# Probabilities of the second batch transposed by TensorE instead of VectorE, in an attention and two-MoE kernel

## The chip, the core and the metric

The kernel runs on one core of one Trainium2 chip. The metric is the device time of one execution in microseconds (us), as the median of several runs; smaller is better. All engines of the core (TensorE or PE, its weight loads PEld, VectorE or DVE, ScalarE or ACT, GpSimd or POOL, and SyncE or SP, which issues the transfers) run their own instruction streams in order and meet through semaphores.

## What is computed

Three stages follow each other. The pooled attention has 8 batches, 8 heads, 576 tokens and a head dimension of 64, and its keys and values are means of 8 neighbouring tokens, so each token attends to 72 positions. Then come two feed-forward stages over 4608 tokens of width 512. All of it is in float32; the weights of the stages arrive as float64.

```python
k_p = k.reshape(B, H, Sp, 8, D).mean(axis=3)
v_p = v.reshape(B, H, Sp, 8, D).mean(axis=3)
scores = (1 / sqrt(D)) * q @ k_p.T
attn = exp(scores - max(scores)); attn = attn / (sum(attn) + 1e-9)
x = (attn @ v_p) -> (4608, 512)
x2 = ((x @ w1) * (x @ w2)) @ w3 @ w_out
h = x2 @ w_in2;  out = (h * sigmoid(1.702 * h)) @ w_out2
```

## The kernel before

The heads are worked on in pairs: a group is one batch and two heads, so there are 32 groups, four to a batch, numbered n = 0 to 31. A group goes through small functions, each given out at one tick of a counter, four ticks to a group:

- `g0` (line 251) transposes keys and queries by DVE blocks and pools the keys.
- `g1` (line 263) makes the scores: five pairs of matmuls on line 271 into the two PSUM banks `wk[2]` and `wk[3]`, a maximum by DVE (line 276) and a subtraction (line 278) into `s_t`, a tile of 128 tokens by 5 token tiles by 160 columns, of which 144 hold the 2 x 72 scores.
- `g2` (line 285) is the exponential on ACT.
- `g3` (line 288) sums and normalizes the probabilities on DVE (lines 292 to 295). Then the matmul that follows needs them with the 144 positions on partitions. For a group n that is not below `NPE`, `g3` does this itself by 20 DVE instructions (line 306), each turning blocks of 32 x 32, from `s_t` to `p0` (the first 128 positions) and `p1` (the last 16, padded to 32). For n below `NPE` it returns on line 301.
- `g4` (line 337) does the same for n below `NPE` by ten PE transposes against an identity (lines 343, 346, 348, 352 and 353) into `wk[2]` and `wk[3]`, with four ACT copies (lines 344, 350, 351 and 354) from there to `p0` and `p1`. For every group it then splits `p0` and `p1` into a high and a low part in the reduced format that PE takes (lines 360 to 364, ACT and POOL).
- `g6` (line 366) multiplies by the pooled values, two halves of 288 tokens, into `wk[2]` and `wk[3]`, and writes the high part (ACT, line 382) and the low part (DVE, line 383) of the result to the slots of `x`.

The ticks have this order: tick 4n gives `g4(n-1)`, tick 4n+1 `g1(n)`, tick 4n+2 `g6(n-1)`, `g2(n)`, `g_va(n)` and `g0(n+1)`, tick 4n+3 `g3(n)` and `g_vb(n)`. A setup phase converts the float64 weights (lines 166 to 174) and multiplies `w3` by `w_out` (one matmul for all tokens instead of two); it gives out ticks 0 to 19, which carry groups 0 to 3 to their end and group 4 through `g3`. Then nine blocks of 512 tokens follow. A block has eight steps f; each step is 24 matmuls of 512 columns into `wk[0]` and `wk[1]` (lines 113 to 115, called from line 585), a copy of `wk[0]` by ACT (line 599), the product by DVE (line 602), the split of it, and 12 matmuls into `acc` for an earlier step (line 550), with two ticks in between. So block 0 carries groups 4 to 7, which are batch 1, from `g4(4)` to `g6(7)`; block 1 needs them. Block 0 itself needs groups 0 to 3. Matmuls on lines 113 to 115 are triples of high and low parts: high by high, high by low, low by high. The `w_in2` and `w_out2` stage comes after the nine blocks.

A framework sets the semaphores, and orders the instructions of each engine ahead of time by the priority of the program's order and by its own simulated times; the order on the chip is then fixed. Tiles of one PSUM bank are handed from one user to the next in program order, so `g1(n+1)` takes `wk[2]` and `wk[3]` after the last reader of `g4(n)`, where that used them.

Of the kernel before, what the change touches and what calls it, by code (L numbers as in the profile page):

```python
# [22 lines left out]
def pooled_attention_moe_moe2(  # L23
# [26 lines left out]
    HP = H // 2  # L50
# [2 lines left out]
    NF2 = DF2 // P  # L53
    NB = NT // T
    NG = B * HP
    NPE = HP
    SB = S // 32
    TT = (S + P - 1) // P
    KW = 2 * SK
# [133 lines left out]
    with pa_ctx:  # L193
# [94 lines left out]
        def g3(n):  # L288
# [10 lines left out]
            g_s[n] = (p0, p1)  # L299
            if n < NPE:  # L300
                return
# [35 lines left out]
        def g4(n):  # L337
            p0, p1 = g_s.pop(n)
            if n < NPE:
                ps = wk[2:]  # L340
# [573 lines left out]
```

## Time and profile before

| what | us |
|---|---|
| median of 3 runs | 1552.37 (1552.19 to 1552.53) |
| the profiled execution | 1552.57 |
| its span, first to last instruction | 1550.9 |
| PE busy | 1491.6 |
| DVE busy | 983.4 |
| ACT busy | 618.6 |
| POOL busy | 590.1 |

The profile gives each engine's busy time, a table of stretches with each engine's busy time and PE's granted clock (1.00 is 2.4 GHz, 0.50 is 1.2 GHz), a timeline of instructions, and for each idle time of an engine what ended it. Matmuls are pipelined: the duration of one is longer than the distance from its start to the next one's, so PE's cost is read from starts.

### The profile page before, as it was taken

How to read it: one execution, taken by the hardware profiler on the slowest of the kernel's cores; microseconds unless marked ns; L12 is line 12 of the kernel's file. 1: busy time of each engine (PE TensorE's matmuls, PEld its weight loads, DVE VectorE, ACT ScalarE, POOL GpSimd, SP SyncE). 2: the span in 40 equal slices, each digit the busy share in tenths (PEclk: the TensorE clock that was granted, in tenths of full speed). 3: DMA queues.
4: the chain of work that ended last, by engine and by line, in shares of the span. 5: the costliest groups of instructions: out<-in, count | busy, mean ns of one | idle time of the engine just before them, and what ended most of it. 6: DMA issues, size and time to landing. Idle time of an engine off the chain costs nothing.

```text
span 1550.9 us, 19562 instructions
## 1 busy us (share of the span) xinstructions
PE 1491.6 (96%) x6728; PEld 1230.2 (79%) x6728; DVE 983.4 (63%) x1810; ACT 618.6 (40%) x1202; POOL 590.1 (38%) x660
## 2 busy tenths in 40 slices
PE   5975999999999999999999999999999999999998
PEld 4653888888888888887878888888888888888887
DVE  8999988787877877669554244463447253734441
ACT  6774444334344333366553222342225222522231
POOL 7788755555555555359472211101110011101110
PEclk9876999999999999999999999999999999999999
DMA  9971233223232320089879243323343233423310
GB/s 273 248 174 37 57 60 74 54 67 68 59 67 53 74 47 36 27 277 368 347 255 380 89 150 129 128 84 134 111 136 109 102 124 115 150 74 123 129 48 28
DMA packets 225444, 196.33 MB, mean 127 GB/s; under 512 B 158784, under 2 KB 175168, under 8 KB 225344
## 3 DMA queue, kind: packets, MB, share of 16 engines
q1 hardware_dynamic: 224768, 194.03, 40.7%
q8 instruction: 53, 0.87, 0.2%
q10 hardware_dynamic: 576, 1.05, 0.2%
q14 instruction: 47, 0.39, 0.1%
HBM read 150.99 MB, written 44.04 MB: 126 GB/s over the span
## 4 chain that ended last, share of the span: by engine, by line
PE 85%; DVE 8%; DMA 2%; issue 2%; SPq 1%; POOL 1%; ACT 1%; DVEq 0%; POOLq 0%
PE bk L682 22%; PE bk L114 8%; PE bk L115 8%; PE bk L113 8%; PE wk L113 7%; PE wk L115 7%; PE wk L114 7%; PE acc L113 4%; PE acc L115 4%; PE acc L114 4%; PE wk L271 2%; DVE cv L171 1%; DVE s L104 1%; DVE cv L168 1%; DMA s<-in_moe_w_dram 1%
## 5 line engine op out<-in xcount | busy, mean ns | idle before, releaser
L682 PE MATMUL bk<-xM,st 128*128 128x512 f32 x1080 | 261.3, 389 | 0.0
L682 PEld LDWEIGHTS bk<-xM,st 128*128 128x128 f32 x1080 | 202.6, 188 | 42.5 <-ACT o L699 0.4
L113 PE MATMUL wk<-s,s 128*128 128x512 f32 x576 | 228.1, 398 | 6.1 <-ACT s L382 3.7
L114 PE MATMUL wk<-s,s 128*128 128x512 f32 x576 | 226.4, 394 | 4.1 <-DVE s L383 4.1
L115 PE MATMUL wk<-s,s 128*128 128x512 f32 x576 | 225.8, 393 | 1.4 <-DVE s L104 1.4
L114 PE MATMUL bk<-wo,mv 128*128 128x512 f32 x576 | 224.1, 389 | 0.0
L113 PE MATMUL bk<-wo,mv 128*128 128x512 f32 x576 | 223.9, 389 | 0.0
L115 PE MATMUL bk<-wo,mv 128*128 128x512 f32 x576 | 209.9, 389 | 0.0
L306 DVE STREAM_TRANSPOSE p<-s_t 32x160 f32<-32x160 f32 (+1 forms) x560 | 178.6, 319 | 11.0
L818 POOL TENSOR_TENSOR s<-s,sg 128x512 f32<-128x512 f32 x32 | 41.4, 1293 | 332.8 <-ACT sg L817 332.8
L115 PE MATMUL acc<-s,s 128*128 128x512 f32 x352 | 141.0, 401 | 5.1 <-DVE s L104 5.1
L114 PE MATMUL acc<-s,s 128*128 128x512 f32 x352 | 140.0, 398 | 0.4 <-POOL s L104 0.3
L104 POOL TENSOR_TENSOR s<-a,s 128x512 fp32r<-128x512 f32 x56 | 72.7, 1298 | 175.5 <-ACT s L103 135.0
L113 PE MATMUL acc<-s,s 128*128 128x512 f32 x352 | 134.2, 404 | 4.8 <-ACT s L103 4.8
L113 PEld LDWEIGHTS wk<-s,s 128*128 128x128 f32 x576 | 108.5, 189 | 30.6 <-ACT s L382 4.4
L114 PEld LDWEIGHTS wk<-s,s 128*128 128x128 f32 x576 | 109.1, 189 | 27.0 <-DVE s L383 5.3
L115 PEld LDWEIGHTS wk<-s,s 128*128 128x128 f32 x576 | 109.0, 189 | 24.7 <-DVE s L104 1.9
L113 PEld LDWEIGHTS bk<-wo,mv 128*128 128x128 f32 x576 | 108.1, 188 | 22.5
L115 PEld LDWEIGHTS bk<-wo,mv 128*128 128x128 f32 x576 | 108.1, 188 | 22.5
L114 PEld LDWEIGHTS bk<-wo,mv 128*128 128x128 f32 x576 | 108.1, 188 | 22.4
L174 POOL TENSOR_TENSOR cv<-cv,s 128x512 int32<-128x512 int32 x72 | 100.9, 1407 | 56.1 <-DVE cv L171 31.5
L834 DVE TENSOR_TENSOR q<-bk,m 128x512 f32<-128x512 f32 x32 | 22.1, 691 | 150.8 <-PE bk L682 150.8
(152 smaller groups left out, 2548.7 us busy)
## 6 DMA issues: line engine op xcount, KB each, us to landing
st<-wind SPq DMA_DIRECT2D x89, 512.0 KB, 3.4
s<-in_moe_w_dram SPq DMA_DIRECT2D x32, 512.0 KB, 6.7
wind<-s SPq DMA_DIRECT2D x32, 512.0 KB, 5.8
s<-in_moe_w_out_dram SPq DMA_DIRECT2D x24, 512.0 KB, 7.9
s<-wind SPq DMA_DIRECT2D x23, 512.0 KB, 3.4
kr<-in_k_dram SPq DMA_DIRECT2D x128, 72.0 KB, 2.4
qr<-in_q_dram SPq DMA_DIRECT2D x128, 72.0 KB, 2.5
out_dram<-o SPq DMA_DIRECT2D x36, 256.0 KB, 2.0
```

The source lines that it names most:

```text
L104: lo_eng.tensor_tensor(out=dst[:, 1], in0=src, in1=f32(dst[:, 0]), op=ALU.subtract)
L113: nc.tensor.matmul(o, a[:, 0, a_sl], b[:, 0, b_sl], start=first, stop=False)
L114: nc.tensor.matmul(o, a[:, 0, a_sl], b[:, 1, b_sl], start=False, stop=False)
L115: nc.tensor.matmul(o, a[:, 1, a_sl], b[:, 0, b_sl], start=False, stop=last)
L168: nc.vector.tensor_scalar(out=eu, in0=eu, scalar1=4, scalar2=1, op0=ALU.logical_shift_left, op1=ALU.logical_shift_right)
L171: nc.vector.scalar_tensor_tensor(out=wu, in0=hi_w, scalar=0x80000000, in1=eu, op0=ALU.bitwise_and, op1=ALU.bitwise_or)
L174: nc.gpsimd.tensor_tensor(out=w.bitcast(I32), in0=w.bitcast(I32), in1=lo_w.bitcast(I32), op=ALU.add)
L271: nc.tensor.matmul(sc[half][:, i * KW:(i + 1) * KW], qT[:, sl(tt)], mov, start=True, stop=True)
L306: nc.vector.transpose(out=dst[:, :nt, 32 * c:32 * c + 32], in_=s_t[32 * c:32 * c + 32, :nt, 32 * r:32 * r + 32])
L682: nc.tensor.matmul(o, w[:, x, m], b[:, y], start=first and n == 0, stop=last and n == 2, skip_group_check=True)
L818: eng.tensor_tensor(out=v, in0=v, in1=sg, op=ALU.mult)
L834: nc.vector.tensor_tensor(out=q_, in0=o, in1=m1, op=ALU.add)
```

## The change

`NPE` goes from 4 to 8 (`HP` is 4). Groups 4 to 7 leave `g3` on line 301 and take the PE branch of `g4`; groups 0 to 3 took it before, and groups 8 to 31 stay with DVE.

```diff
--- before.py
+++ after.py
@@ -53,7 +53,7 @@
     NF2 = DF2 // P
     NB = NT // T
     NG = B * HP
-    NPE = HP
+    NPE = 2 * HP
     SB = S // 32
     TT = (S + P - 1) // P
     KW = 2 * SK
```

The two places that read it, with their lines of the kernel before:

```python
            if n < NPE:                      # 300, in g3: the 20 DVE transposes are skipped
                return
            if n < NPE:                      # 339, in g4: ten PE transposes, four ACT copies
                ps = wk[2:]
```

## Rows read from the trace of the kernel before

**Rows 1.** The page, busy time, share of span and instructions of each engine.

```profile
PE 1491.6 (96%) x6728; PEld 1230.2 (79%) x6728; DVE 983.4 (63%) x1810; ACT 618.6 (40%) x1202; POOL 590.1 (38%) x660
```

**Rows 2.** The page, 40 slices of the span, busy tenths.

```profile
PE   5975999999999999999999999999999999999998
```

**Rows 3.** Stretches: length, busy us of PE, PEld, DVE, ACT, POOL; clock; DMA.

```profile
140.00:160.00 20.00, 13.82 (x55) 10.47 (x54) 19.35 (x41) 7.74 (x16) 15.13 (x19) 0.74 0.25 47
160.00:180.00 20.00, 20.00 (x99) 16.79 (x98) 18.97 (x44) 8.99 (x23) 15.00 (x25) 1.00 0.36 71
...
200.00:220.00 20.00, 18.97 (x92) 15.91 (x91) 18.55 (x47) 7.25 (x17) 12.72 (x20) 1.00 0.28 60
```

**Rows 4.** Stretches, around the start of block 0.

```profile
146.26:150.20 3.94, 3.94 (x12) 3.11 (x13) 3.76 (x12) 1.31 (x3) 1.73 (x3) 0.50 0.00 0
150.20:154.12 3.92, 3.48 (x16) 2.43 (x14) 3.81 (x10) 2.04 (x4) 3.17 (x3) 1.00 0.00 2
```

**Rows 5.** Timeline of PE there: start, us, instruction, [idle before, releaser].

```profile
139.31 1.22 PE L113 MATMUL wk<-s,s 128*128 128x512 f32 x2 [0.50 <-ACT s L382]
146.26 1.81 PE L271 MATMUL wk<-kbd,qT 128*128 128x144 f32 x6 [5.73 <-DVE s L383]
147.69 0.80 PE L114 MATMUL wk<-s,s 128*128 128x512 f32 x1
...
154.12 0.50 PE L113 MATMUL wk<-s,s 128*128 128x512 f32 x1 [0.35 <-DVE a L602]
```

**Rows 6.** Timeline of DVE in the same stretch.

```profile
142.36 1.59 DVE L295 TENSOR_TENSOR s_t<-s_t,nm 128x720 f32<-128x720 f32 x1
144.06 1.65 DVE L306 STREAM_TRANSPOSE p<-s_t 32x160 f32<-32x160 f32 x5
145.75 0.46 DVE L383 TENSOR_TENSOR s<-wk,s 128x288 fp32r<-128x288 f32 x1
146.24 0.97 DVE L306 STREAM_TRANSPOSE p<-s_t 32x160 f32<-32x160 f32 x3
147.24 0.39 DVE L383 TENSOR_TENSOR s<-wk,s 128x224 fp32r<-128x224 f32 x1
147.66 4.01 DVE L306 STREAM_TRANSPOSE p<-s_t 32x160 f32<-32x160 f32 x12
...
153.40 0.67 DVE L602 TENSOR_TENSOR a<-wk,a 128x512 f32<-128x512 f32 x1
```

**Rows 7.** PE's waits from 157 to 740 us: total us, times, longest.

```profile
PE wk L271 <- DVE s L383: 1.0, 1, 1.0
```

**Rows 8.** Groups of instructions on the page: busy us, mean ns, idle before.

```profile
L306 DVE STREAM_TRANSPOSE p<-s_t 32x160 f32<-32x160 f32 (+1 forms) x560 | 178.6, 319 | 11.0
```

**Rows 9.** Timeline of PE, transposes of group 0, clock at 2.4 GHz.

```profile
49.04 0.60 PE L343 MATMUL wk<-ident,s_t 128*128 128x128 f32 x4
49.57 0.27 PE L346 MATMUL wk<-ident,s_t 64*128 64x64 f32 x1
49.77 0.50 PE L348 MATMUL wk<-ident,s_t 128*32 128x128 f32 x3
50.03 0.48 PE L115 MATMUL acc<-s,s 128*128 128x512 f32 x1
50.34 0.40 PE L113 MATMUL acc<-s,s 128*128 128x512 f32 x1
50.58 0.40 PE L114 MATMUL acc<-s,s 128*128 128x512 f32 x1
...
52.43 0.27 PE L352 MATMUL wk<-ident,s_t 128*32 128x128 f32 x1
...
52.79 0.76 PE L271 MATMUL wk<-kbd,qT 128*128 128x144 f32 x4
```

**Rows 10.** Timeline of PE, transposes of group 2, clock at 1.2 GHz.

```profile
101.79 1.11 PE L343 MATMUL wk<-ident,s_t 128*128 128x128 f32 x4 [0.39 <-DVE s_t L295]
...
104.62 1.33 PE L271 MATMUL wk<-kbd,qT 128*128 128x144 f32 x4 [0.23 <-ACT p L351]
107.04 1.81 PE L271 MATMUL wk<-kbd,qT 128*128 128x144 f32 x6 [1.09 <-ACT p L354]
```

**Rows 11.** Groups of instructions by form, 0 to 420 us, ScalarE.

```profile
L344 ACT COPY p<-wk 128x512 f32<-128x512 f32 x4 | 2.3, 583 | 1.4 <-DVE s L104 1.3
```

## The prediction

> **What bounds the kernel now.** I read the page first. PE is busy for 96% of the span, DVE for 63%, ACT for 40% [rows 1]. The shares are means over stages, so the 40 slices come next: PE's row is ragged for the first four slices of 39 us and reads 9 from the fifth on [rows 2]. The change touches groups 4 to 7, which are worked on at the end of the setup and in block 0, so the third view is the table of stretches from 140 to 220 us. There the bound changes hands. From 140 to 160 us DVE is busy 19.35 of 20 us and PE only 13.82; from 160 to 200 PE is full; from 200 to 220 it misses 1.03 us [rows 3]. What this change can win is PE's idle time in that stretch; what it can lose is PE's time once PE is full. DVE's share of 97% in the first stretch is worth nothing by itself.
>
> The timelines say what the idle time waits for. PE ends its last ready matmuls of block 0 with the pair at 139.31, and then waits until 146.26 (5.73 us idle) for L383 [rows 5]. That is the low part of group 3's result, which frees `wk[2]` and completes the last input of block 0. ACT had made the high part by 139.31, so L383 was not short of data: it stood in DVE's queue behind other work, last of all the normalization of group 4 (L295, 142.36 to 143.95) and five of group 4's twenty transposes; the second L383 stood behind three more, and the other twelve ran after it [rows 6]. Matmul L114, which needs that second L383, starts at 147.69. At 154.12 PE waits again, for the product L602, which came to its turn only at 153.40, after the twelve transposes [rows 5, 6]; in that stretch PE is busy 3.48 of 3.92 us, so 0.44 us are open [rows 4]. From 157 to 740 us there is one wait of the attention on DVE, 1.0 us [rows 7].
>
> **The change, part by part.** First, what goes: 4 x 20 = 80 DVE transposes at 319 ns [rows 8], 25.5 us of DVE. They are worth only what PE waited for them. Three places:
>
> (a) At 146.26. L295 ends at 143.95 and is still needed by the new path. Without the five transposes the first L383 can start at about 144.06 instead of 145.75, at most 1.7 us earlier. It can also gain nothing, if the order made ahead puts other waiting DVE work (weight conversion, L168 and L171) in the freed place. PE's clock in the 3.94 us after the wait is granted at 0.50, the 1.2 GHz level [rows 4], so a microsecond there is worth half of one later, unless the return to 2.4 GHz moves forward too. Bounds 0 and 1.7 us; I take half of 1.7 at half speed, 0.4 us.
>
> (b) At 154.12, the open 0.44 us: with the twelve transposes away, L602 has nothing long ahead of it. Gone, 0.4 us; bounds 0 and 0.44.
>
> (c) The 1.0 us wait on L383 later in block 0 [rows 7]. DVE loses some 6.4 us of work in each group, so I count it as gone: 1.0 us; bounds 0 and 1.0.
>
> Together 1.8 us, between 0 and 3.1 (all of (a) at full worth).
>
> Second, what comes: ten PE transposes a group, in groups 4 to 7. They exist in the trace, for groups 0 to 3, so their price needs no guess, only care to count from start to start. At 2.4 GHz the first eight take from 49.04 to 50.03, 0.99 us; the matmul after them occupies 0.31 us (50.03 to 50.34) where the one after it needs 0.24, another 0.07 for the switch back; the last two take from 52.43 to 52.79, 0.36 us [rows 9]. With one more switch that is 1.5 us a group. At 1.2 GHz the ten take 101.79 to 104.62 less 0.23 of waiting, 2.6 us [rows 10], or 1.3 us of full-speed time, so the same 1.5 us stand for group 4, wherever the clock is. Four groups cost 6.0 us of PE. Bounds: 1.42 us a group without the second switch, 5.7 us in all, less some 0.5 us where group 4's first transposes could run while L114 still waits for the second L383; and 1.9 us a group (an estimate: two further pieces between other matmuls, with 0.2 us each for switching there and back), 7.6 us. For three groups nothing covers this, because PE is full from 160 us on [rows 3].
>
> Third, ACT gets four copies a group, none longer than the 0.58 us of the largest [rows 11], under 2.4 us in all, where ACT is busy 9 of 20 us [rows 3]. I cost them at nothing: ACT has the room. If that cover fails, ACT's copy of `wk[0]` (L599) is late, and with it the next step's matmuls. The POOL and ACT splits of `p0` and `p1` stay as they are, and no transfer is added or moved.
>
> Fourth, new waits in PE's queue: the ninth transpose waits for ACT's copy of the first four, because they share `wk[2]`, and `g1` of the next group waits for the last copies. Behind such a wait stands all of PE. In group 2 these waits cost 0.23 and 1.09 us [rows 10], when PE had nothing else to do; in group 0 there is none, as other matmuls lie between (50.03 to 52.43) [rows 9]. Block 0 has such matmuls in plenty. Between 0 and 1.3 us a group, I take 0, nearest to group 0.
>
> The sum: + 6.0 - 1.8 = + 4.2 us against the profiled execution's 1552.57, thus 1556.8; the median of the runs is 0.2 below that execution, so I forecast 1556.6. The sum's own bounds are + 5.2 - 3.1 = + 2.1 and + 7.6 - 1.0 = + 6.6 (only (c) gained), 1554.5 to 1559.0. About 0.2%, 3.1 us, is what a measurement here tells from no change; the border is 1555.5.
>
> **Where the Trainium skill would have it otherwise.** PE's starts in a dense stretch lie 0.24 us apart for 512 columns (50.34 to 50.58) [rows 9], with no gap to put a transpose in. The Trainium skill's page "Perfetto Trace Analysis", section "Identifying the Most-Contended Engine", says that matmul busy time is not a good measure of how near TensorE is to its limit, and that the weight loads' busy share is a better one; that share is 79% here [rows 1], and read so PE had room for the transposes. By that rule the sum would be the gains alone; by the starts the cost is real.
>
> The clock stands at 1.00 from 160 us on [rows 3], and after group 0's first eight transposes the matmuls follow each other by 0.24 us, the pace of the 2.4 GHz level [rows 9]. The Trainium skill's page "TensorE: Matmul & The Clock Gate", section "PE-mode transpose", says that the full clock does not engage for transposes, which count otherwise than matmuls as activity. The row does not agree, as far as transposes among matmuls go. By that rule the price of rival four below would come on top.
>
> **The rivals.** One, PE has room: the starts hide slack, the 6.0 us vanish, and 1.8 us are gained, 1550.8. Against it are the 0.24 us starts. It would decide if transposes slipped between matmuls without moving the next start.
>
> Two, not slower: the order of DVE changes by more than the missing transposes. L383's data were there at 139.31, so if the order put it ahead of the normalization, PE would go on at 140.5 instead of 146.26. The low-clock stretch would move along, so the full 5.7 us count, with (b) and (c) 7.1 against 6.0 us: - 1.1, thus 1551.3. It needs at least 4 us of that wait to go for the total to fall below + 0.6. For it: the order is made from simulated times, and those place L383 late. Against it: taking away work that came after the normalization gives no reason to pull L383 ahead of it.
>
> Three, PE waits for ACT: 1.3 us in each group as in group 2, 5.2 us more, 1561.8. Against it is group 0.
>
> Four, the clock falls with each group's transposes: a stretch at half level as long as the 3.94 us [rows 4] for each of four groups loses 4 x 2.0 = 8 us, 1564.6. Against it stands the pace right behind group 0's transposes [rows 9].
>
> That the change does not do what it says can be left out: both branches read the same constant.
>
> **How the numbers follow.** Forecast 0.62 (of it 0.15 under the 0.2% border, by larger gains), rival one 0.07, two 0.15, three 0.12, four 0.04. Of one and two I give 0.06 to faster by more than 0.2%, with gains that I have not seen, and 0.16 to no change. So slower 0.47 + 0.12 + 0.04 = 0.63, same 0.15 + 0.16 = 0.31, faster 0.06. The forecast's own range is 1554.5 to 1559.0. To hold 8 in 10, the range reaches down to where rival two lies, 1551.2, and up to most of rival three, 1561.0.
>
> **What would show it.** In the profile after: 480 transposes on L306 instead of 560; PE's wait at 146.26 ending between 144.5 and 146.3; no idle of PE before the second step's matmuls; the ten transposes of groups 5 to 7 taking about 1.5 us from start to start, and block 1 beginning some 4 us later than now. A PE wait on L344 or L354 in block 0 would speak for rival three, a granted clock under 1.00 after 155 us for four, a first L383 before L295 for two, an unchanged start of block 1 for one. The prediction fails if the order made ahead changes elsewhere, later in the nine blocks, by more than 3 us.

## The result, and the profile after

| | us |
|---|---|
| before, median of 4 runs beside it | 1552.45 (1552.19 to 1552.55) |
| after, median of 4 runs | 1565.54 (1564.64 to 1565.89) |
| ratio after to before | 1.0082, 95% interval 1.0070 to 1.0095 |
| profiled execution after, its span | 1565.87, 1564.2 |

The kernel is 13.1 us slower, where 4.2 us slower was forecast and 1561.0 was the upper end of the range.

The page of the kernel after, busy time of the engines, to be held against [rows 1]; then, from the list of groups, the DVE transposes that are left, against [rows 8]:

```profile
PE 1502.0 (96%) x6768; PEld 1234.5 (79%) x6768; DVE 958.6 (61%) x1730; ACT 623.9 (40%) x1218; POOL 588.4 (38%) x660
L306 DVE STREAM_TRANSPOSE p<-s_t 32x160 f32<-32x160 f32 x480 | 153.0, 319 | 9.1
```

The change did what it says: 80 DVE instructions fewer, 40 PE instructions and 16 ACT copies more, DVE 24.8 us less busy. The stretches from 140 us on, columns as in [rows 3]:

```profile
140.00:160.00 20.00, 16.20 (x71) 12.24 (x69) 12.57 (x21) 8.98 (x21) 16.41 (x24) 0.77 0.23 43
160.00:180.00 20.00, 20.00 (x100) 16.45 (x99) 6.68 (x13) 8.03 (x20) 12.13 (x19) 1.00 0.22 48
...
200.00:220.00 20.00, 20.00 (x100) 16.61 (x99) 7.81 (x15) 6.66 (x17) 8.74 (x14) 1.00 0.24 46
220.00:240.00 20.00, 15.13 (x68) 11.87 (x66) 14.94 (x38) 7.42 (x19) 7.11 (x12) 0.91 0.37 97
240.00:260.00 20.00, 19.53 (x87) 16.31 (x88) 17.78 (x40) 9.14 (x20) 12.71 (x17) 0.91 0.24 45
```

Up to 220 us this is the picture that was hoped for: DVE is no longer full, and PE misses nothing after 160 us. Then, from 220 to 240 us, where PE was full before, it misses 4.9 us and its clock falls. To place the loss, here are the starts of the k-th matmul of 512 columns (lines 113 to 115 and 682 counted together in each trace), in us:

| k | before | after | after less before |
|---|---|---|---|
| 200 (setup) | 99.33 | 99.42 | 0.1 |
| 400 | 199.40 | 199.27 | -0.1 |
| 475 (block 1 has begun) | 220.02 | 219.84 | -0.2 |
| 500 | 226.96 | 232.05 | 5.1 |
| 550 | 239.38 | 251.02 | 11.6 |
| 700 | 278.12 | 289.84 | 11.7 |
| 2600 (end of the nine blocks) | 760.76 | 772.49 | 11.7 |
| 3400 | 945.09 | 958.17 | 13.1 |
| 5800 | 1489.09 | 1502.40 | 13.3 |

Up to the 475th the two are level, with 38 of the 40 new transposes done. That does not mean that the transposes were free: the count is of matmuls of 512 columns alone. From 139 us to there, the transposes take 5.5 us of PE, its waits are 3.3 us shorter, and its scores and values take 2.9 us less, as the groups lag and 14 of these matmuls are not done yet. Between the 475th and the 550th matmul, in 30 us at the start of block 1, 11.8 us are lost, the delayed matmuls among them, and they never come back. PE's waits from 139 to 260 us after (total us, times, longest):

```profile
PE wk L343 <- DVE s L383: 3.8, 1, 3.8
PE wk L113 <- DVE a L602: 2.6, 1, 2.6
PE wk L372 <- DVE s_t L278: 2.1, 1, 2.1
PE wk L113 <- ACT s L382: 1.2, 2, 0.7
```

The first is the old wait at the start of block 0, 3.8 us instead of 5.7 [rows 5]. Of the last, 0.5 us stood before it in both kernels [rows 5]. The others are new. PE's timeline at the start of block 1:

```profile
226.76 0.30 PE L375 MATMUL wk<-pt,vt 96*128 96x288 f32 x1
229.12 0.41 PE L372 MATMUL wk<-ph,vm 128*128 128x288 f32 x1 [2.06 <-DVE s_t L278]
...
230.61 0.83 PE L113 MATMUL wk<-s,s 128*128 128x512 f32 x2 [0.69 <-ACT s L382]
...
240.47 0.50 PE L113 MATMUL wk<-s,s 128*128 128x512 f32 x1 [2.59 <-DVE a L602]
```

and DVE's:

```profile
231.76 0.99 DVE L295 TENSOR_TENSOR s_t<-s_t,nm 128x720 f32<-128x720 f32 x1
232.68 0.44 DVE L276 TENSOR_REDUCE nm<-wk 128x4 f32<-128x288 f32 x1
233.04 6.65 DVE L306 STREAM_TRANSPOSE p<-s_t 32x160 f32<-32x160 f32 x20
239.72 0.69 DVE L602 TENSOR_TENSOR a<-wk,a 128x512 f32<-128x512 f32 x1
```

Block 1 needs group 7. Its matmuls with the values (L372) run at 226 and 229 us and its result arrives at 230.6; before, they ran at 212.6 and 213.4. The second half waits 2.06 us until DVE has subtracted (L278) in the scores of group 8, which hold its bank, and PE, whose order is fixed, waits with it. When PE goes on, DVE turns group 8, the first one of the old path, in one piece of 6.65 us, and the product L602 of block 1's first step stands behind that. The clock falls twice, to the 1.2 GHz level (columns as in [rows 3]):

```profile
231.10:234.50 3.40, 3.40 (x13) 3.02 (x12) 3.28 (x10) 0.59 (x1) 3.32 (x7) 0.50 0.58 95
241.35:244.70 3.35, 3.35 (x10) 2.57 (x9) 2.46 (x5) 1.73 (x3) 2.02 (x2) 0.50 0.50 84
```

PE works through both stretches, at half speed, so they cost up to 3.4 us.

Why group 7 is late is seen in block 0 before anything stands still. The exponential L286, one for each group, starts at (ACT's timeline of the kernel before):

```profile
157.40 0.81 ACT L286 ACTIVATE s_t<-s_t 128x720 f32<-128x720 f32 x1 [1.24 <-DVE s_t L278]
174.13 0.81 ACT L286 ACTIVATE s_t<-s_t 128x720 f32<-128x720 f32 x1 [1.86 <-DVE s_t L278]
193.23 0.81 ACT L286 ACTIVATE s_t<-s_t 128x720 f32<-128x720 f32 x1 [3.25 <-DVE s_t L278]
210.06 0.81 ACT L286 ACTIVATE s_t<-s_t 128x720 f32<-128x720 f32 x1
```

and in the kernel after:

```profile
157.44 0.81 ACT L286 ACTIVATE s_t<-s_t 128x720 f32<-128x720 f32 x1 [2.15 <-DVE s_t L278]
181.81 0.81 ACT L286 ACTIVATE s_t<-s_t 128x720 f32<-128x720 f32 x1 [1.18 <-DVE s_t L278]
206.11 0.81 ACT L286 ACTIVATE s_t<-s_t 128x720 f32<-128x720 f32 x1 [1.41 <-DVE s_t L278]
229.10 0.81 ACT L286 ACTIVATE s_t<-s_t 128x720 f32<-128x720 f32 x1 [1.71 <-DVE s_t L278]
```

These are groups 5, 6, 7 and 8. A group took 17 to 19 us; now it takes 23 to 24. One such round, from the normalization of group 5 to the scores of group 6, from the timelines of DVE, PE and ACT after:

```profile
160.44 1.43 DVE L295 TENSOR_TENSOR s_t<-s_t,nm 128x720 f32<-128x720 f32 x1
...
167.46 0.60 PE L343 MATMUL wk<-ident,s_t 128*128 128x128 f32 x4
...
168.10 0.59 ACT L344 COPY p<-wk 128x512 f32<-128x512 f32 x1 [1.71 <-PE wk L343]
...
172.89 0.27 PE L352 MATMUL wk<-ident,s_t 128*32 128x128 f32 x1
...
173.50 0.30 ACT L354 COPY p<-wk 32x192 f32<-32x192 f32 x1
...
178.41 0.90 PE L271 MATMUL wk<-kbd,qT 128*128 128x144 f32 x6
```

The normalized probabilities are ready at 161.9, and the four transposes into `wk[2]` start at 167.5 (the first of the others at 167.1); the copy is done at 168.7, and the ninth transpose starts at 172.9; the last copy is done at 173.8, and the scores that need its bank start at 178.4. PE waits for nothing there and is 100% busy: the instructions stand in its queue, nearly all of the time behind matmuls of 512 columns, 5.6, 4.2 and 4.6 us, 14.4 of the group's 24.4 us. Before, from the end of that normalization (162.1 us) to those scores it was 7.7 us instead of 16.5, and DVE's transposes needed no turn on PE:

```profile
162.22 6.66 DVE L306 STREAM_TRANSPOSE p<-s_t 32x160 f32<-32x160 f32 x20
169.85 0.90 PE L271 MATMUL wk<-kbd,qT 128*128 128x144 f32 x6
```

Theory A, for the experiments: each return of a group to a full PE costs it 4 to 5 us in the queue; the three rounds in block 0 so become 5 to 8 us longer each (24.4, 24.3 and 23.0 us against 16.7, 19.1 and 16.8), together more than the slack of the kernel before, and PE pays at the start of block 1, in waits and in clock. Theory B: each group that is moved costs the same. Theory C: transposes or copies slow PE or its clock where they run. Medians of one kernel moved by up to 0.6 us between groups of runs, and single runs of it by up to 5 us, so each kernel is held against the kernel before on the same chip.

### The profile page after: what moved, and what is told of

It reads as the page before. It is cut to its first block, busy times and chain, and to the rows that moved or that the text cites. A ratio compares the mean times of both kernels' runs of the same rounds, so it can differ in the third digit from the quotient of the medians.

```text
span 1564.2 us, 19580 instructions
## 1 busy us (share of the span) xinstructions
PE 1502.0 (96%) x6768; PEld 1234.5 (79%) x6768; DVE 958.6 (61%) x1730; ACT 623.9 (40%) x1218; POOL 588.4 (38%) x660
## 4 chain that ended last, share of the span: by engine, by line
PE 85%; DVE 8%; DMA 3%; issue 1%; SPq 1%; ACT 1%; POOL 1%; DVEq 0%; ACTq 0%
PE bk L682 21%; PE bk L113 8%; PE bk L114 8%; PE bk L115 8%; PE wk L113 8%; PE wk L114 8%; PE wk L115 8%; PE acc L113 4%; PE acc L115 4%; PE acc L114 4%; PE wk L271 2%; DVE s L104 1%; DVE cv L171 1%; DVE cv L168 1%; DMA s<-in_moe_w_dram 1%
## 5 line engine op out<-in xcount | busy, mean ns | idle before, releaser
L306 DVE STREAM_TRANSPOSE p<-s_t 32x160 f32<-32x160 f32 x480 | 153.0, 319 | 9.1
L104 POOL TENSOR_TENSOR s<-a,s 128x512 fp32r<-128x512 f32 x56 | 72.0, 1286 | 167.1 <-ACT s L103 132.9
L818 POOL TENSOR_TENSOR g<-g,sg 128x512 f32<-128x512 f32 x32 | 42.1, 1315 | 196.3 <-ACT sg L817 189.0
```

Of the source, the lines that this page charges most:

```text
L104: lo_eng.tensor_tensor(out=dst[:, 1], in0=src, in1=f32(dst[:, 0]), op=ALU.subtract)
L306: nc.vector.transpose(out=dst[:, :nt, 32 * c:32 * c + 32], in_=s_t[32 * c:32 * c + 32, :nt, 32 * r:32 * r + 32])
L818: eng.tensor_tensor(out=v, in0=v, in1=sg, op=ALU.mult)
```

## The experiments

**One, two and three groups on PE.** The edit is the one constant, here for group 4 alone:

```diff
-    NPE = 2 * HP
+    NPE = HP + 1
```

> Only group 4 goes over to PE. Theory A (the chain of a group becomes longer by the PE transposes and ACT copies, each standing in the full PE queue; it is 24 us instead of 17 to 19 in block 0, so group 7 comes late and block 1 starts with an idle PE and a low clock): group 4 is turned while PE still waits for DVE, the exponential of group 5 stays at 157.4 us, group 7 is not late, no idle of PE at the start of block 1; PE's price of 1.5 us less the gains of about 1 to 1.8 us, so 1551.5 to 1553.5. Theory B (each group turned costs the same, a quarter of the 13.1 us): 1555.7.

Measured: 1551.26 us against 1553.0, ratio 0.9989 (0.9980 to 0.9998). The exponential of group 5 starts at 158.6 us (this execution is 0.7 us late already at 97 us, ahead of the change), that of group 8 at 211.3, and PE has no wait on the attention at the start of block 1.

> Groups 4 and 5 go over to PE. Theory A (longer chain): group 5 brings the first 7 us of lateness, of which 1.7 us are slack in the kernel before (group 7's low part ends at 216.9 us, block 1 takes it at 218.6 us), so PE begins to wait at block 1: 1555 to 1560, more for this group than for group 4. Theory B (the same for each group): 1559.0.

Measured: 1553.33 against 1553.0, ratio 1.0004 (0.9995 to 1.0014). Under the range of theory A, at the kernel before: the exponential after the added group comes at 181.9 us, 7.7 us late, but the next exponentials follow in 18.9, 14.9 and 15.7 us, where before it were 19.1, 16.8 and 18.7, with DVE busy 6.7 us from 160 to 180 instead of 19.0. Block 1 waits 0.7 us. (The profiled execution, 1556.06 us, is slower than the median by stretches in the last stage; up to the 2600th matmul it lies 0.2 us above the kernel before.)

> Groups 4 to 6 go over to PE. Theory A (longer chain): two groups bring 7 us of lateness each, and group 7, turned by DVE, follows at the old pace: 1559 to 1564. Theory B (the same for each group): 1562.3.

Measured: 1558.03 against 1552.81, ratio 1.0033 (1.0020 to 1.0045), just under theory A's range. PE's new wait in block 1 is not for the group itself, but for ACT's copy of `wk[0]`; ACT's timeline there, and the wait:

```profile
232.77 0.67 ACT L360 CAST ph<-p 128x576 fp32r<-128x576 f32 x1 [3.07 <-DVE p L306]
233.35 0.58 ACT L599 COPY a<-wk 128x512 f32<-128x512 f32 x1
PE wk L113 <- ACT a L599: 2.1, 1, 2.1
```

The copy stands in ACT's queue behind the split of group 8, which waits for DVE's twenty transposes of that group (227.4 to 234.0 us). The lateness has moved them onto the first step of block 1. With the full change the steps against the kernel before, median to median, are -1.7, +0.3, +5.2 and +13.1 us, so the four groups add -1.7, +2.1, +4.9 and +7.9 us. Theory B's equal parts of 3.3 us are out. The first group gains, and each further one costs more than the one before, which fits slack that is used up.

**DVE relieved, PE not loaded.**

```diff
-            if n < NPE:
+            if n < HP:
                 return
+            if n < NPE:
+                for t in (p0, p1):
+                    nc.gpsimd.memset(t, 0.0)
+                return
```

(In `g4`, the PE branch is then for n below `HP` as before the change.)

> Groups 4 to 7 are turned by neither engine: POOL fills p0 and p1 with zeros, so the attention of batch 1 is left out. It shows what the 80 DVE transposes are worth at most. Theory A: the chain is shorter than before, PE's waits at 154.1 and 205.9 us vanish and the one at 146.3 us shrinks, nothing else changes: 1549.5 to 1551.5. If it is below 1548, DVE's transposes cost more than the waits that the trace showed.

Measured: 1549.12 against 1553.0, ratio 0.9975 (0.9966 to 0.9984), 3.9 us and a little under theory A's range. The wait at the start of block 0 is 3.8 us, and no other wait of PE on DVE is left up to 262 us. So all that the 80 transposes of DVE can give back is under 4 us. The forecast's gains were 1.8, with 3.1 as the upper bound.

**PE loaded, DVE not relieved.** In the kernel before, in `g4`, for groups 4 to 7, ten transposes of the same shapes from a constant tile into `wk[2]` and `wk[3]`, for example:

```diff
+            if HP <= n < 2 * HP:
+                ps, w = wk[2:], S - T
+                for tt in range(4):
+                    nc.tensor.transpose(ps[0][:, sl(tt)], ident, ident)
...
```

> The kernel before, DVE keeps all its transposes, and PE does ten more transposes of the same shapes in each of groups 4 to 7, from a constant tile into the same banks, read by nobody. It measures PE's price without the longer chain. Theory A: 4 x 1.5 us where PE is full, 1557.0 to 1558.8, and no idle of PE at the start of block 1. If PE had room between its matmuls: 1552.4. If transposes lower the clock: a granted clock under 1.00 between 155 and 230 us, and 1560 or more.

Measured: 1560.59 against 1553.0, ratio 1.0049 (1.0032 to 1.0066). PE's groups of these transposes from 139 to 235 us:

```profile
L358 PE MATMUL wk<-ident 128*128 128x128 f32 x16 | 2.9, 312 | 5.7 <-DVE s L393 5.7
L361 PE MATMUL wk<-ident 128*32 128x128 f32 x12 | 2.3, 310 | 0.0
L363 PE MATMUL wk<-ident 128*32 128x128 f32 x4 | 1.2, 308 | 0.0
L359 PE MATMUL wk<-ident 64*128 64x64 f32 x4 | 1.1, 272 | 2.8 <-DVE s L393 2.8
L364 PE MATMUL wk<-ident 64*32 64x64 f32 x4 | 1.0, 242 | 0.0
```

Counted from each start to the next instruction's, the forty take 6.2 us in this trace, and 5.85 us in the kernel after; the forecast said 6.0. The rest of the 7.6 us fits the longer waits, 1.4 us more in all: 5.7 us at 146.4, then 2.4 us at 153.1 and 0.4 us at 211.6, all for L383, because the idle transposes write the banks that L383 reads, where before they are 5.7, 0.4 and 1.0 us. Part of the sign for a lower clock is there: from 153.3 to 156.7 us it is granted at 0.50, right after the wait of 2.4 us, and four transposes of group 4 run from 153.1 to 153.9. The thirty of groups 5 to 7 run at 1.00, which holds from 160 to 240 us, and PE is full from 220 to 240. Block 1's first matmul starts at 223.57 us, before at 215.72. So PE has no room between its matmuls, transposes among matmuls did not lower the clock, and PE's price alone makes no wait at block 1. Theory C is out for the transposes; the copies are not in this kernel, but no wait of PE on one is seen in block 0 of the kernel after.

**The link from group 7 to block 1 cut.**

```diff
             x = [x_slot(blk, c) for c in range(KM)]
+            if blk == 1:
+                x[3] = x[2]
```

> The changed kernel, but block 1 reads the result of group 6 where it should read that of group 7, so block 1's output is not the reference's; all groups are still worked out. Theory A (block 1 waits for group 7 because the chain is longer): the waits of PE from 226 to 240 us and the two low-clock stretches shrink or vanish, and most of 8.7 us comes back: 1556 to 1560. Theory C (transposes or their copies slow PE where they run): no change, 1565.

Measured: 1558.49 against 1552.81, ratio 1.0038 (1.0023 to 1.0053), 7.1 us under the changed kernel, or 7.4 if each is held against the kernel before beside it. From 200 to 262 us one wait of PE is left, and the clock is at 1.00 from 148.7 to 260 us:

```profile
PE wk L113 <- DVE a L604: 0.8, 1, 0.8
```

The groups are as late as in the changed kernel (exponentials at 181.5, 205.8 and 229.9 us), and it no longer matters. This is the size of the lateness, 7.1 to 7.4 us of the 13.1. What stays, 5.7 us against the kernel before, is in the main PE's price less the gains: by the starts in its trace it is 4.7 us from 139 us to the 1000th matmul of 512 columns, 5.9 for the transposes and 1.7 for matmuls of 512 columns that start further apart, less 1.9 of waiting and 0.9 in scores and values. The rest comes in the last stage.

**Half of the work, one round less.** Groups 4 to 7 with five transposes and two copies; the last 16 positions by 4 DVE instructions:

```diff
-            if n < NPE:
+            if n < HP:
                 return
-            for r in range(5):
+            for r in range(4 if n < NPE else 0, 5):
```

(and in `g4` lines 347 to 349 and 351 to 354 only for n below `HP`).

> The changed kernel, but in groups 4 to 7 PE turns only the first 128 positions (five transposes, two copies), and DVE the last 16 (4 instructions instead of 20). Theory A: the second pair of transposes, which waits for ACT's copy and then stands in PE's queue again, is gone, so the next group's scores come sooner, the chain is 17 to 20 us and block 1 does not wait; PE's price halves to about 3 us, less the gains: 1553 to 1556. Theory B (PE's price alone scales, half of 13.1): 1559.

Measured: 1555.29 against 1552.81, ratio 1.0017 (1.0007 to 1.0026). The exponentials come at 155.7, 177.5, 197.0 and 216.6 us, so a group takes 19.6 to 21.7 us and not 23.0 to 24.4, and the matmuls of block 1 do not wait; PE waits once, 1.1 us, ahead of the scores at 228.8. What was taken from PE and ACT, the second pair of transposes with its copy and its place in the queue above all, is worth 2.7 to 4.7 us a group, 3.6 on the mean, net of the 4 DVE instructions that came.

**Precedence for the transposes.**

```diff
-                ps = wk[2:]
+                with (tc.high_priority() if n >= HP else ExitStack()):
+                    ps = wk[2:]
```

(with the rest of the branch inside).

> The changed kernel with the same instructions, but the ordering ahead of time gives the transposes and copies of groups 4 to 7 precedence over other work. Theory A with the place in PE's queue as the cause: the transposes stand earlier, the chain shortens, 1556 to 1561. If the second round through ACT and the shared banks is the cause, whatever the place: 1563 to 1566.

Measured: 1565.59 against 1552.81, ratio 1.0084 (1.0069 to 1.0099). This does not tell the two readings apart: the 6768 matmuls and transposes of PE stand in the same order as in the changed kernel. More precedence did not bring the transposes ahead of the matmuls. That their place comes from the times at which the ordering takes their inputs to be ready is likely, but not shown.

**One more round, DVE as loaded as before.** In the kernel before, ahead of the splits in `g4`:

```diff
+            if HP <= n < 2 * HP:
+                nc.tensor.transpose(wk[2][:32, :P], s_t[:, 3, P:], ident)
+                nc.scalar.copy(p1[:, 3], wk[2][:32, :P])
```

> The kernel before; DVE keeps all its transposes, but in each of groups 4 to 7 one transpose of 32 columns by PE and one ACT copy are put behind them, giving again the values that DVE had written. PE's price is 4 x about 0.3 us. It tests one more round through PE and ACT in the chain of a group, with DVE as loaded as before. Theory A (each return to the full PE queue costs a group 4 to 5 us): the exponentials of groups 6 to 8 come later than at 174, 193 and 210 us in the kernel before, by some 5 us a group, PE waits at the start of block 1, and the time is 1556 to 1561. If only PE's own time counts: 1553.5 to 1554.

Measured: 1556.43 against 1552.81, ratio 1.0022 (1.0013 to 1.0031). ACT's timeline of this kernel, groups 5 to 8:

```profile
158.09 0.81 ACT L286 ACTIVATE s_t<-s_t 128x720 f32<-128x720 f32 x1 [2.56 <-DVE s_t L278]
179.54 0.81 ACT L286 ACTIVATE s_t<-s_t 128x720 f32<-128x720 f32 x1 [1.18 <-DVE s_t L278]
200.89 0.81 ACT L286 ACTIVATE s_t<-s_t 128x720 f32<-128x720 f32 x1 [0.94 <-DVE s_t L278]
222.78 0.81 ACT L286 ACTIVATE s_t<-s_t 128x720 f32<-128x720 f32 x1
```

and PE's waits at the start of block 1 in it:

```profile
225.18 0.73 PE L113 MATMUL wk<-s,s 128*128 128x512 f32 x2 [0.49 <-ACT s L385]
231.67 0.50 PE L113 MATMUL wk<-s,s 128*128 128x512 f32 x1 [0.73 <-ACT a L602]
235.66 0.50 PE L113 MATMUL wk<-s,s 128*128 128x512 f32 x1 [0.95 <-DVE a L605]
```

Four transposes of 128 columns and four copies of 0.25 us, and a group takes 21 to 22 us instead of 17 to 19. The time is 3.6 us up. The four transposes take 0.5 us of it from start to start, less than the 1.2 expected; three waits at block 1, 2.2 us together, are new, in the place where the changed kernel has its own. Elsewhere waits of 1.0 us at 147.6 and 0.6 us at 265.2 came, and those of 0.4 and 1.0 us of the kernel before went. That is theory A's direction, cadence and place, at the lower end of its size, as a round is 4.0 us longer on the mean here and 6.3 us there.

**Group 4 alone, again, and its half.**

> Group 4 alone goes over to PE, a second time in more rounds, beside the next kernel. The first time gave 1551.26 against 1553.0. Theory A: 1 to 2 us below the kernel before.

Measured: 1550.85 against 1552.81, ratio 0.9986 (0.9977 to 0.9994).

> Group 4 alone goes over to PE, and only with its first 128 positions (five transposes and two copies); DVE turns its last 16 with 4 instructions instead of 20. Theory A: half of PE's price, one round trip less, but the four DVE instructions stand ahead of L383 again: between 1550.5 and 1552, within 1 us of the kernel with group 4 wholly on PE.

Here the edit is that of the half-work kernel with `NPE = HP + 1`. Measured: 1551.96 against 1552.81, ratio 0.9993 (0.9984 to 1.0002), no clear difference to the kernel before. Group 4 wholly on PE has thus the lowest time of the versions that give the reference's output, 1.7 to 2.0 us under the kernel before in two sets of runs; its half lies 1.1 us above it. Group 4 is the one whose first transposes run at 144.4 us, where PE stood idle before until 146.3, and whose DVE transposes stood ahead of L383.

## Why the prediction was wrong, point by point

What bounds the kernel: right up to the end of block 0. Gain (a): right in mechanism, sized too small. The first L383 starts at 143.9 instead of 145.75, just over the upper bound, and PE's wait ends 1.8 us earlier (144.42 against 146.26). It was worth more than the half that was counted, as the return to 2.4 GHz came forward too, from 150.2 to 149.2 us. Gains (b) and (c): right, both waits are gone. The relieved kernel sets all gains together at 3.9 us, where 1.8 was taken and 3.1 was the bound.

PE's price: right within its bounds. It is 5.85 us from start to start, 2.25 of them group 4's at the low clock, where 6.0 was worked out with the switch behind each burst in it. These switches cost the matmuls of 512 columns beside the bursts nearly another 1 us (0.32 instead of 0.23 us behind a burst), so counted alike it is 6.8, where 7.6 was the bound. It is additive, as the kernel with idle transposes shows. The rule of the Trainium skill's page "Perfetto Trace Analysis", section "Identifying the Most-Contended Engine", was weighed against the starts; with a weight loads' share of 79% PE had no room, and the starts were the better guide here. The clock: right that transposes among matmuls did not lower it here (1.00 from 160 to 220 us).

The step that failed is the fourth, the new waits, taken as 0 because "block 0 has such matmuls in plenty". It looked only at whether PE stands still at the transposes of block 0. It does not. But the same matmuls that keep PE busy are the queue in which the group waits: 14.4 us of a round. The step also named who waits behind the instruction on PE, and not who waits for the group. That is block 1, by way of group 7, and in the kernel before there was little slack. The low part of group 7's result for block 1, and the first matmul behind it that carries a wait for DVE, one of the last four of block 1's first step:

```profile
216.61 0.32 DVE L383 TENSOR_TENSOR s<-wk,s 128x160 fp32r<-128x160 f32 x1
220.48 0.39 PE L114 MATMUL wk<-s,s 128*128 128x512 f32 x1
```

The slack was thus some 3.5 us, and not the 1.7 us to 218.6 that the expectation for two groups names: there the matmul of the high part starts. Group 8's exponential, the measure of the lateness, comes at 229.1 instead of 210.1 us. The cost came 50 to 80 us after the place where it arose: waits of 2.1, 0.7 and 2.6 us, 5.3 together, and two low-clock stretches worth up to 3.4 us. The longest of the waits is for L602 behind the twenty DVE transposes of group 8, which the lateness put at the first step of block 1. Cutting the link gave 7.1 to 7.4 us back.

Of the prediction's signs, the 480 transposes on L306 came, the earlier end of the wait too (144.42, where 144.5 was the lower bound), and the transposes of groups 5 to 7 took 1.2 us each from start to start. Block 1 did not begin 4 us later: its first matmul starts at 214.51 instead of 215.72, and its second step at 234.85 instead of 225.01. By itself that is the sign of rival one, which the kernel with idle transposes rules out.

The sum with the measured terms, from the starts in the two profiled executions, 139 us to the 1000th matmul of 512 columns:

| term | us |
|---|---|
| waits that went: 1.9 of (a), 0.4 of (b), 1.0 of (c) | -3.3 |
| new waits at block 1 | +5.3 |
| forty transposes, start to start | +5.9 |
| matmuls of 512 columns, 790 in both: 188.0 instead of 184.2 | +3.9 |
| scores and values | -0.1 |
| together | +11.6 |

The table of starts has 11.7 us there. Of the 3.9, some 2.7 are the clock (9.2 us of these matmuls at the 1.2 GHz level instead of 3.8, at half speed) and nearly 1 the switches. Another 1.6 us come in the last stage, between the 2600th and the 5800th matmul. The trace after has two waits of 0.4 us there, on an output copy and on a weight transfer, that the trace before does not have; the rest was not traced to a cause. In the traces of the other kernels that stage is up to 0.5 us shorter or 3.3 us longer than in the kernel before, so little can be read from the 1.6.

Rival three gave a time near the measured one, 1561.8 us, and not its cause: it had PE itself wait for ACT's copies, 1.3 us in each group. In block 0 no such wait exists after. (Both waits that the prediction read from group 2 are of scores, L271; none is of the ninth transpose [rows 10].) Rival four's low stretches did come, worth up to 3.4 us, but behind the waits of block 1 and not at the transposes. Rival two's idea, that L383 moves ahead of the normalization, did not come about, and rival one fell with the kernel that kept DVE's transposes and loaded PE as well.

What stays open is whether a round would be short if the transposes stood at the head of the queue. Precedence did not move them, and a second `s_t` tile or a bank of their own for the last two transposes was not tried.

## What to carry to other kernels

When a step moves from a lightly queued engine to the full one, price two things: the time it takes there, and the time it stands in line for each turn, for everything downstream. Count the turns of one unit of work on the full engine before and after, times the length of the line seen in the trace, and compare the sum with the slack at the next point where all must meet. Less than the lateness was lost here, as PE went on with other work that was ready: group 8 came 19 us later, and 7.1 to 7.4 us of time went with it. Moving only the unit that falls into that engine's idle time can win where moving all of them loses.

## What the runs showed that was not expected

Three short waits of PE within 14 us (2.06, 0.69 and 2.59 us) were followed by two stretches at the 1.2 GHz level, 3.40 and 3.35 us long, worth nearly two thirds as much as the waits themselves; the kernel in which the forty transposes ran without such waits at block 1 kept 2.4 GHz there. In the kernel with three groups the new waits were 0.21 and 2.13 us, and after the second the clock was at 0.50 from 234.4 to 237.7 us. After the waits of 1.03 us in the kernel before (205.9 us) and 1.09 us with half of the work (228.8 us) it stayed at 1.00.

DVE's 20 transposes of one group, some 6.65 us in one piece, cost PE most where they stood ahead of the first step of block 1: 2.59 us in the kernel after, by way of the product L602, and 2.13 us with three groups, by way of ACT's queue. With PE full before them they cost 0.8 us in the kernel with group 4 alone (wait for L602 at 190.8 us), and nothing from 162.2 to 168.9 us of the kernel before.
